# Value products of a pooled attention regrouped from four runs into three, with one block transpose and two copies moved in their queues

## The chip, the cores and the metric

The kernel runs on one core of a Trainium2 chip. The metric is the device time of one execution in microseconds (us). Five engines work side by side, each through its own queue in order: PE (matrix products; its weight loads appear as a row of their own, PEld), DVE (vector), ACT (activation functions), POOL (general), and SP, which here only issues DMAs. They meet through semaphores.

## What is computed

The first stage is attention with pooled queries for 4 batches and 8 heads: 576 queries, 1152 keys, 64 numbers per head. Two mixing stages with matrix products follow, which the change does not touch.

```
q_pool = q.reshape(B, H, S // factor, factor, D).mean(axis=3)
scores = scale * np.matmul(q_pool, k.transpose(0, 1, 3, 2))
scores = scores - np.max(scores, axis=-1, keepdims=True)
attn = np.exp(scores)
attn = attn / (np.sum(attn, axis=-1, keepdims=True) + 1e-09)
return np.matmul(attn, v).astype(np.float32)
...
x = _moe_ref(x=x, **moe_kwargs)
return _moe2_ref(x=x, **moe2_kwargs)
```

## The kernel before, in words

The 32 heads are taken in 16 pairs. A pair has nine **tiles** of 128 query rows by 1152 keys: `TILES` (L277) gives head and block of rows; the fifth tile (index 4) mixes the last 64 rows of both heads. Each tile goes through the same steps:

- `scores` (L291): six products on PE (nine for the mixed tile) into one of two score buffers `SC`, of three PSUM banks each, which the tiles use in turn.
- `smax` (L312): the maximum of each row, on DVE.
- `sexp` (L327): the exponential on ACT, into one of two buffers `e`, with the row sums beside it.
- The exponentials have to be turned, keys onto partitions. Tiles 0 to 3 are turned in blocks on DVE (`turn_blocks`, L351) into the buffer `blk`, and 16 DMAs (`move_blocks`, L357) put the blocks in place in the buffer E. These are the **near** tiles. Tiles 4 to 8, the **far** ones, are turned on PE (`fill`, L382): one block into a bank of the score buffer ("o"), four into the bank TY ("y"), four into the bank TX ("x"). Copies by ACT (o, y) and DVE (x) put them into the buffer M (`take`, L392).
- `pv_part` (L410) multiplies the turned exponentials by the values. The near product of a pair (E, 256 columns) and the far product (M, 320 columns) are nine **parts** each, a part being one product for each head; the trace shows every such product as two PE records, so a part is four records. Each product sums in one PSUM bank, and `pv_copy` (L424) copies the sum out of it on ACT.

The order is written by hand: a loop over **slots** (L657), one for each tile, emits everything, and an engine's queue follows that order. Slot n of a pair emits, for tiles 0 to 3: what `at_gap` has put there, a block transpose, the exponential of tile n+1, what `at_mid` has put there, the scores and then the maximum of tile n+2, the value products of the plan, and what `at` has put there. For tiles 4 to 8 it emits the "o" transpose and its copy, the exponential of tile n+1, the scores of tile n+2, the "y" and "x" transposes, the maximum of tile n+2, and the "x" copy.

So scores run two tiles ahead of the slot and exponentials one. Slots 0 to 3 of a pair also hold the value products of the pair before it: `shares` (L340) sets how many parts lie in which slot. They are emitted behind the scores of tile n+2. In the text below S2 to S8 are the scores of tiles 2 to 8, and S0', S1', S2' those of the next pair's first tiles, which are emitted in slots 7, 8 and (next) 0. One more table, `PREP` (L47), puts the preparation of the next pair's queries and keys (POOL, ACT) and its loads into slots; its entry 'qd' is `q_double` (L256), a copy on ACT.

Of the rest, three steps matter. `norm0` to `norm3` and `spread` invert the row sums (POOL, then a reciprocal and a small transpose on DVE), and send them through device memory to the buffer `rb`; `norm2` (L465) multiplies the value sums by them on POOL, once both copies of `pv_copy` and `rb` are there. Behind `norm2` on POOL stand the low halves of the next pair's keys (`k_lo`, L268), which S0' and S2' read. And on SP's queue the DMAs of `blk` stand behind those of `rb`.

Of the kernel before, what the change touches and what calls it, by code (L numbers as in the profile page):

```python
# [26 lines left out]
NP = NB * NH // 2  # L27
KT = S // 128
# [15 lines left out]
NORM = 9  # L44

PREP1 = ((1, 0, 'kh'), (1, 0, 'qs'), (1, 0, 'qm'), (1, 2, 'qo', 0), (2, 0, 'kt', 0), (2, 2, 'kl', 0, 0), (3, 0, 'kl', 0, 1), (4, 0, 'qo', 1), (4, 2, 'kt', 1), (5, 0, 'kl', 1, 0), (5, 2, 'kl', 1, 1), (5, 2, 'lk'), (5, 2, 'lq'), (5, 2, 'qd', 0), (7, 2, 'qd', 1), (20, 1, 'lv'))
PREP = ((-1, 2, 'qs'), (0, 0, 'qm'), (0, 0, 'qo', 0), (0, 2, 'qo', 1), (1, 1, 'lk'), (1, 1, 'kh'), (2, 0, 'lq'), (2, 1, 'qd', 0), (2, 2, 'kt', 0), (3, 1, 'kt', 1), (3, 1, 'qd', 1), (4, 2, 'kl', 0, 0), (5, 0, 'kl', 0, 1), (6, 0, 'kl', 1, 0), (6, 2, 'kl', 1, 1), (20, 1, 'lv'))  # L47

PIECES = {"a": ((1, 2), ((2, 2), (2, 2), (2, 2)), (9, 2), 14, 15), "x": ((1, 2), ((2, 2), (2, 2), (2, 2)), (3, 2), 5, 7)}
LATE = 5  # L50
# [12 lines left out]
def attn_moe_kernel(ctx: ExitStack, tc: tile.TileContext, qT, kT, vP, muk, mur, wk, wv, wr, wth, wtr, wti, wch, ident, out):  # L63
# [94 lines left out]
    def attention(first):  # L158
# [11 lines left out]
        TX = psV.tile([128, 512], F32, tag="tx", name="tx")  # L170
        TY = psV.tile([128, 512], F32, tag="ty", name="ty")
# [3 lines left out]
        def bank(eng, ins, *banks):  # L175

            ins = ins.ins
            need = []
            for x in banks:
                e, i = owner.get(x, (eng, None))  # L180
                if e != eng and all(i is not y for y in need):
                    need.append(i)
                owner[x] = (eng, ins)
            for e in ("pe", "act", "dve"):
                if e != eng:
                    tc.declare_no_dep(ins, group="sc_" + e, keep=[i for i in need], reason="ordered bank by bank")
            for i in need:
                tc.add_manual_dep(ins, i.name, sync, reason="bank")
            tc.add_to_no_dep_group("sc_" + eng, ins)
# [30 lines left out]
        kts, vns, rss, raws, qs = {}, {}, {}, {}, {}  # L220
# [58 lines left out]
        def quick(P):  # L279
            return P > 0  # L280

        def by_block(n):
            return quick(n // KT) and n % KT < 4
# [3 lines left out]
        def tile_of(n):  # L287
            P, t = divmod(n, KT)
            return (TILES if P else FIRST)[t]
# [22 lines left out]
        def smax(n):  # L312
            m = sm.tile([128, 1], F32, tag="m", name="m")
            if n < THIRDS:

                m3 = sm.tile([128, 4], F32, tag="m3", name="m3")
                for c in range(3):
                    r = dve.tensor_reduce(m3[:, c:c + 1], scs[n][:, c, 0:384], axis=AX.X, op=ALU.max, negate=True)
                    bank("dve", r, (n % 2, c))
                dve.tensor_reduce(m, m3[:, 0:3], axis=AX.X, op=ALU.min)  # L320
                ms[n] = m
                return
            r = dve.tensor_reduce(m, scs[n][:, :, 0:384], axis=AX.XY, op=ALU.max, negate=True)  # L323
            bank("dve", r, *[(n % 2, c) for c in range(3)])
            ms[n] = m

        def sexp(n):  # L327
            P, t = divmod(n, KT)
            if t == 0:
                rss[P] = RS[P % 3]  # L330
            sc, m = scs[n], ms.pop(n)
            e = es_[n] = ep.tile([128, 3, 384], F32, tag="e", name="e", bufs=2)
            x = tile_of(n)
            t = 4 if x is None else 5 * x[0] + x[1]
            r = act.activation(e, sc[:, :, 0:384], AF.Exp, bias=m, scale=1.0, accum_out=rss[P][:, t:t + 1])  # L335
            bank("act", r, *[(n % 2, c) for c in range(3)])
# [3 lines left out]
        def shares(P):  # L340

            if P == NP - 1:
                return ((8, 9),), ((8, 9),)
            return ((9, 5), (10, 4)), ((11, 5), (12, 4))

        pvs = {}

# [3 lines left out]
        def turn_blocks(n):  # L351

            h, t = tile_of(n)
            out = BLK.rearrange("p m (h k t i) -> p h t k m i", h=2, k=KT, t=2)[:, h, t]
            dve.transpose(out, es_[n].rearrange("p a b -> p (a b)").rearrange("p (k m i) -> p k m i", k=KT, m=4))  # L355
# [49 lines left out]
        def take_rest():  # L405
            for n in rest:
                take(n, "y")
            rest.clear()

        def pv_part(k, x):  # L410

            P, g = k
            w = groups[g][1]
            j = (x + 3) % KT
            if x == 0:
                pvs[k] = TX if k == (NP - 1, 0) else TY
            for h in range(2):
                e = Es[k][:, h, j]
                out = pvs[k][64 * h:64 * h + 64, :w]
                if g == 0 and quick(P):  # L420
                    out = out.rearrange("p (a q) -> p a q", a=4)
                pe.matmul(out, lhsT=vns[P][:, h, j], rhs=e, start=(x == 0), stop=(x == KT - 1))  # L422
# [47 lines left out]
        NT = NP * KT  # L470
# [3 lines left out]
        def at(slot, fn, *args):  # L474
            sched.setdefault(slot, []).append((fn, args))
# [3 lines left out]
        def at_mid(slot, fn, *args):  # L479
            mids.setdefault(slot, []).append((fn, args))  # L480
# [3 lines left out]
        def at_gap(slot, fn, *args):  # L484
            gaps.setdefault(slot, []).append((fn, args))
# [3 lines left out]
        for P in range(NP):  # L489
            for g, when in sorted(enumerate(shares(P)), reverse=P == NP - 1):  # L490
                j = 0
                for o, m in when:
                    n = min(P * KT + o, NT)
                    plan.setdefault(n, []).extend(((P, g), j + x) for x in range(m))
                    j += m
                assert j == KT
                if P == NP - 1:
                    at(n, pv_copy, (P, g))
                else:
                    at_gap(n + 1, pv_copy, (P, g))  # L500
            if P == NP - 1:
                for step in (norm0, norm1, norm3):
                    at(NT - 1, step, P)
                at_mid(NT, spread, P)
                at(NT, norm2, P)
            else:
                at(P * KT + NORM, norm0, P)
                at(P * KT + NORM + 1, norm1, P)
                at_mid(P * KT + NORM + 2, norm3, P)
                at(P * KT + NORM + 2, spread, P)  # L510
                at_mid(P * KT + NORM + 4, norm2, P)
            if quick(P):
                at(P * KT + 2, move_blocks, P)

        def run_pv(s):
            for k in plan.pop(s, []):
                pv_part(*k)
# [3 lines left out]
        def prep_sched(P):  # L521
            base = (P - 1) * KT
            for o, hook, name, *args in (PREP if P > 1 else PREP1):
                if P + (name[0] == "l") < NP and (P > 1 or base + o >= 3 or name != "lv"):
# [132 lines left out]
        for s in range(NT + 1):  # L657
            for fn, args in gaps.pop(s, []):
                fn(*args)
            take_rest()  # L660
            if s < NT and by_block(s):
                if s % KT < 3:
                    turn_blocks(s)
                sexp(s + 1)
                if s % KT == 2:
                    turn_blocks(s + 1)
            elif s < NT:
                fill(s, "o")
                take(s, "o")
                if s + 1 < NT:  # L670
                    sexp(s + 1)
            for fn, args in mids.pop(s, []):
                fn(*args)
            if s + 2 < NT:
                scores(s + 2)
            if s < NT and not by_block(s):
                fill(s, "y")
                fill(s, "x")
                rest.append(s)
            if s + 2 < NT:  # L680
                smax(s + 2)
            if s < NT and not by_block(s):
                take(s, "x")
                if s in plan:
                    take_rest()
            run_pv(s)
            for fn, args in sched.pop(s, []):
                fn(*args)
            if s == NT - 1:
                es3.close()  # L690
                next(follow)
                es2.close()
                next(follow)
                next(follow)
            if s == NT:
                next(follow)
                es.close()
                next(follow)
# [494 lines left out]
    with tc.manual_schedule():  # L1193
        dve.memset(hpi, math.pi / 2)
        WR = []
        first = weight_pieces("wr", wr, 512, in_dram, 512) + weight_pieces("wk", wk, 512, in_dram, 512)
        first += weight_pieces("wv", wv, 512, in_dram, 512)[:8 - LATE]
        attention(first)
# [39 lines left out]
```

## Time and profile before

| | |
|---|---|
| time, median of 3 runs | 919.16 us (919.1 to 920.14) |
| the profiled execution | 919.25 us, of which 917.5 us is the span from its first to its last instruction |
| PE busy (modelled) | 901.8 us, 98% of the span |
| PEld, DVE, ACT, POOL busy | 781.5, 688.4, 542.5, 597.4 us (85, 75, 59, 65%) |
| granted PE clock | 0.998 of full speed |
| attention stage | to about 428 us; then the two mixing stages |

PE is put down as busy for nearly the whole span, but the end of a PE record is modelled, and a run of products that waits for something shows it in the starts, not in the busy share. The starts are therefore read below, within one pair. The rows come from the pair whose S2 starts at 239.61 us; the same stretch recurs in 15 pairs.

### The profile page before, as it was taken

The numbers are of one execution on the slowest core, as the hardware profiler recorded it, in microseconds if no ns is written. First come the engines' busy times: TensorE is split into PE (matmuls) and PEld (weight loads), VectorE is DVE, ScalarE is ACT, GpSimd is POOL, SyncE is SP. The second block draws the span as 40 slices with busy tenths as digits, with TensorE's granted clock in tenths as the row PEclk, the third lists the DMA queues.
The fourth block names the chain that finished last, engine by engine and source line by source line (L and its number), as shares of the span: only waits on it lengthen the run. The fifth ranks groups of instructions, "written<-read, shape, count | busy, mean of one in ns | idle before, by whom it ended". The sixth has DMA issues, their size and how long they took to land.

```text
span 917.5 us, 17359 instructions
## 1 busy us (share of the span) xinstructions
PE 901.8 (98%) x6292; PEld 781.5 (85%) x6292; DVE 688.4 (75%) x965; ACT 542.5 (59%) x1133; POOL 597.4 (65%) x662
## 2 busy tenths in 40 slices
PE   8999999999999999999889999999999999999998
PEld 6677777777777777777889999999999999999998
DVE  7888888888888888882589888888758663676712
ACT  7777777777777777764665565555454442443320
POOL 7976777777887777764386565656567475665631
PEclk9999999999999999999999999999999999999999
DMA  7268876777778877659603333333507100010001
GB/s 237 86 180 240 225 211 188 220 215 210 212 207 233 239 208 201 157 166 325 257 2 125 95 103 104 97 99 113 188 1 253 46 27 27 1 53 1 27 26 52
DMA packets 58773, 129.74 MB, mean 141 GB/s; under 512 B 10752, under 2 KB 29888, under 8 KB 58688
## 3 DMA queue, kind: packets, MB, share of 16 engines
q1 hardware_dynamic: 58688, 128.64, 47.1%
q8 instruction: 49, 0.80, 0.4%
q14 instruction: 36, 0.29, 0.1%
HBM read 70.46 MB, written 22.17 MB: 101 GB/s over the span
## 4 chain that ended last, share of the span: by engine, by line
PE 89%; ACT 4%; DVE 3%; POOL 2%; DMA 1%; issue 1%; SPq 0%; DVEq 0%; ACTq 0%; POOLq 0%
PE sc L302 17%; PE ty L422 15%; PE ps L1130 12%; PE ps L852 11%; PE ps L833 10%; PE ps L1149 6%; PE ps L1076 5%; PE ps L802 3%; PE ty L388 3%; PE tx L388 3%; PE sc L388 2%; DVE m L323 1%; ACT e L335 1%; PE ps L1034 1%; DMA rb<-scr 1%
## 5 line engine op out<-in xcount | busy, mean ns | idle before, releaser
L323 DVE TENSOR_REDUCE m<-sc 128x1 f32<-128x1152 f32 x138 | 185.8, 1346 | 48.6 <-PE sc L302 46.8
L335 ACT ACTIVATE e<-sc,m 128x1152 f32<-128x1152 f32 x144 | 176.3, 1225 | 60.8 <-DVE m L323 56.1
L302 PE MATMUL sc<-kt,q 128*128 128x384 f32 (+1 forms) x864 | 192.9, 351 | 3.1 <-ACT M L399 1.7
L302 PEld LDWEIGHTS sc<-kt,q 128*128 128x128 f32 (+1 forms) x864 | 147.1, 191 | 24.0 <-issue 13.8
L1130 PE MATMUL ps<-b,a 128*128 128x288 f32 x816 | 111.2, 295 | 0.0
L1130 PEld LDWEIGHTS ps<-b,a 128*128 128x128 f32 x816 | 109.3, 188 | 0.6
L833 PE MATMUL ps<-x,a 128*128 128x288 f32 x768 | 105.1, 298 | 2.4 <-ACT g L815 2.4
L833 PEld LDWEIGHTS ps<-x,a 128*128 128x128 f32 x768 | 103.7, 191 | 2.7 <-ACT g L815 2.6
L852 PE MATMUL ps<-k,b 128*128 128x288 f32 x768 | 103.5, 295 | 0.0
L852 PEld LDWEIGHTS ps<-k,b 128*128 128x128 f32 x768 | 102.0, 188 | 0.3
L201 POOL TENSOR_TENSOR kt<-kn,kh 64x576 fp32r<-64x576 f32 (+1 forms) x64 | 87.5, 1386 | 2.4
L355 DVE STREAM_TRANSPOSE blk<-e 128x1152 f32<-128x1152 f32 x60 | 81.6, 1360 | 7.4 <-ACT e L335 7.4
L422 PE MATMUL ty<-M,vn 128*64 128x320 f32 x576 | 84.4, 438 | 0.2 <-ACT M L399 0.2
L422 PEld LDWEIGHTS ty<-M,vn 128*64 128x64 f32 x576 | 38.7, 136 | 36.3 <-issue 3.8
L468 POOL TENSOR_TENSOR xt<-xt,rb 128x576 f32<-128x576 f32 x16 | 21.9, 1370 | 73.0 <-ACT xt L432 67.9
L820 POOL TENSOR_TENSOR k<-h,k 128x288 fp32r<-128x288 f32 x64 | 59.1, 939 | 12.4 <-ACT k L819 12.1
L422 PE MATMUL ty<-E,vn 128*64 128x256 f32 x540 | 64.9, 385 | 0.0
L836 DVE TENSOR_TENSOR h<-h 128x288 f32<-128x288 f32 x64 | 42.2, 662 | 21.9 <-ACT h L835 21.2
L1094 ACT ACTIVATE q<-q 128x512 f32<-128x512 f32 x18 | 11.4, 632 | 78.1 <-DVE q L1091 78.1
L802 PE MATMUL ps<-x,blk 128*128 128x288 f32 x384 | 53.3, 296 | 3.4 <-POOL x L782 2.9
L399 DVE COPY M<-tx 128x512 f32<-128x512 f32 x80 | 54.5, 681 | 1.8 <-PE tx L388 1.8
L782 POOL TENSOR_TENSOR x<-t,x 128x288 fp32r<-128x288 f32 x52 | 44.6, 875 | 16.9 <-ACT x L781 16.4
(147 smaller groups left out, 1748.6 us busy)
## 6 DMA issues: line engine op xcount, KB each, us to landing
E<-blk SPq DMA_DIRECT2D x240, 144.0 KB
vn<-vP SPq DMA_DIRECT2D x16, 576.0 KB
kn<-kT SPq DMA_DIRECT2D x15, 576.0 KB
qn<-qT SPq DMA_DIRECT2D x15, 576.0 KB
b<-wtk SPq DMA_DIRECT2D x9, 576.0 KB
rb<-scr SPq DMA_DIRECT2D x32, 144.0 KB
out<-xt SPq DMA_DIRECT2D x32, 144.0 KB
cv<-wk SPq DMA_DIRECT2D x8, 512.0 KB
```

The lines of the kernel that those rows point to most:

```text
L201: engines[e].tensor_tensor(out, x, hi.bitcast(F32), ALU.subtract)
L302: r = pe.matmul(sc[0:m, c, 0:384], lhsT=x, rhs=k[:, 384 * c:384 * c + 384], start=(i == 0), stop=(i == len(ops) - 1),)
L323: r = dve.tensor_reduce(m, scs[n][:, :, 0:384], axis=AX.XY, op=ALU.max, negate=True)
L335: r = act.activation(e, sc[:, :, 0:384], AF.Exp, bias=m, scale=1.0, accum_out=rss[P][:, t:t + 1])
L355: dve.transpose(out, es_[n].rearrange("p a b -> p (a b)").rearrange("p (k m i) -> p k m i", k=KT, m=4))
L388: r = pe.transpose(ps[:, 128 * j:128 * j + 128], flat[:, 128 * k:128 * k + 128], idn)
L422: pe.matmul(out, lhsT=vns[P][:, h, j], rhs=e, start=(x == 0), stop=(x == KT - 1))
L802: pe.matmul(pss[d], lhsT=WR[k][:, w, 128 * d:128 * d + 128], rhs=x[k][:, c], start=(k == 0 and n == 0), stop=(k == 3 and n == 2))
L820: pool.tensor_tensor(q[:, 1], h, q[:, 0].bitcast(F32), ALU.subtract)
L833: pe.matmul(ps, lhsT=WK[k, f // 4][:, w, 128 * (f % 4):128 * (f % 4) + 128], rhs=x[k][:, c], start=(k == 0 and n == 0), stop=(k == 3 and n ...
L852: pe.matmul(pss[d], lhsT=WV[f][:, w, 128 * d:128 * d + 128], rhs=k2[f][:, c], start=(f == 0 and n == 0), stop=(f == 7 and n == 2))
L1130: pe.matmul(pss[d], lhsT=zs[j][z][:, 128 * d:128 * d + 128], rhs=WTK[min(j, 8)][:, w, cs], start=(m == 0 and n == 0), stop=(m == 8 and n = ...
```

## The change

- **Value products.** `shares` gives, for all pairs but the last, near parts 6 and 3 in slots 0 and 1 (5 and 4 before), and far parts 3 and 6 in slots 1 and 2 (5 and 4 in slots 2 and 3 before). Slot 3 has none any more. The far product now sums in bank TX, the near one in TY; before, both used TY. The last pair stays as it was.
- **Copies of the value sums.** `pv_copy` moves from the head of a slot to behind that slot's exponential: the near copy within slot 2, the far copy from slot 4 to slot 3.
- **Third block transpose.** The transpose of tile 2 moves from slot 2 to the end of slot 1, behind the maximum of tile 3.
- **`PREP`.** The second copy of `q_double` moves from the middle of slot 3 to the end of slot 2.

```diff
-PREP = (... (3, 1, 'kt', 1), (3, 1, 'qd', 1), (4, 2, 'kl', 0, 0), ...)
+PREP = (... (3, 1, 'kt', 1), (2, 2, 'qd', 1), (4, 2, 'kl', 0, 0), ...)
...
-            return ((9, 5), (10, 4)), ((11, 5), (12, 4))
+            return ((9, 6), (10, 3)), ((10, 3), (11, 6))
...
-                pvs[k] = TX if k == (NP - 1, 0) else TY
+                pvs[k] = TX if g == (P < NP - 1) else TY
...
-                    at_gap(n + 1, pv_copy, (P, g))
+                    at_mid(n + 1, pv_copy, (P, g))
...
-                if s % KT < 3:
+                if s % KT < 2:
                     turn_blocks(s)
                 sexp(s + 1)
                 if s % KT == 2:
                     turn_blocks(s + 1)
...
             if s + 2 < NT:
                 smax(s + 2)
+            if s < NT and by_block(s) and s % KT == 1:
+                turn_blocks(s + 1)
```

On PE, from the last product of S4 (the mixed tile) to S6, each row is a line, an operation, its output and inputs, and a count; L302 are scores, L422 value products, L388 transposes. Before:

```order
L302 MATMUL sc_120<-kt,q_0_1_125 128x384
L422 MATMUL ty<-M,vn 64x320 x10
L302 MATMUL sc_121<-kt,q_0_0_124 128x384 x6
L422 MATMUL ty<-M,vn 64x320 x8
L388 MATMUL sc_120<-idn,e 128x128
```

The far product lay half before and half behind S5 (the row of six). Now:

```order
L302 MATMUL sc_120<-kt,q_0_1_125 128x384
L422 MATMUL tx<-M,vn 64x320 x12
L302 MATMUL sc_121<-kt,q_0_0_124 128x384 x6
L388 MATMUL sc_120<-idn,e 128x128
L302 MATMUL sc_120<-kt,q_0_0_124 128x384 x6
```

All that is left of the far product lies before S5, and the "o" transpose of tile 4 follows S5 directly. One slot earlier PE now has six near and six far products behind S3, where eight near ones were.

On ACT, from the exponential of tile 3 to that of tile 5 (L335 exponential, L258 `q_double`, L432 copy of a value sum, L399 copy of transposes), before:

```order
L335 ACTIVATE e,rs_138<-sc_120,m 128x1152
L258 CAST q_0_0_124<-q_0_0_124 64x1152
L335 ACTIVATE e,rs_138<-sc_121,m 128x1152
L258 CAST q_0_1_125<-q_0_1_125 64x2x576
L432 COPY xt_69<-ty 128x320
L399 COPY M<-sc_121 128x2x64
L335 ACTIVATE e,rs_138<-sc_120,m 128x1152
```

and now, where the near copy stands behind the first of these exponentials:

```order
L432 COPY xt_69<-ty 128x4x2x32
L258 CAST q_0_0_124<-q_0_0_124 64x1152
L258 CAST q_0_1_125<-q_0_1_125 64x2x576
L335 ACTIVATE e,rs_138<-sc_121,m 128x1152
L432 COPY xt_69<-tx 128x320
L399 COPY M<-sc_121 128x2x64
L335 ACTIVATE e,rs_138<-sc_120,m 128x1152
```

Both `q_double` copies are ahead of the exponential of tile 4, and the copies of value sums are each behind an exponential.

On DVE, from the maximum of tile 3 to that of tile 5 (L323 maximum, L355 block transpose, L446 and L447 the reciprocal and its small transpose, L133 to L141 conversion of a weight), before:

```order
L323 TENSOR_REDUCE m<-sc_120 128x1
L446 RECIPROCAL r_141<-r_141 128x10
L447 STREAM_TRANSPOSE rt<-r_141 128x32
L355 STREAM_TRANSPOSE blk<-e 128x9x4x32 x2
L323 TENSOR_REDUCE m<-sc_121 128x1
L133 TENSOR_SCALAR cv<-cv 128x512
L137 SCALAR_TENSOR_TENSOR cv<-cv 128x512
L141 SCALAR_TENSOR_TENSOR cv<-cv 128x512
L323 TENSOR_REDUCE m<-sc_120 128x1
```

and now:

```order
L323 TENSOR_REDUCE m<-sc_120 128x1
L355 STREAM_TRANSPOSE blk<-e 128x9x4x32
L446 RECIPROCAL r_141<-r_141 128x10
L447 STREAM_TRANSPOSE rt<-r_141 128x32
L355 STREAM_TRANSPOSE blk<-e 128x9x4x32
L323 TENSOR_REDUCE m<-sc_121 128x1
```

The only step that moved on DVE is one block transpose, past the reciprocal and its transpose.

## Rows read from the trace of the kernel before

**Rows 1.** The page's chain that ended last, its shares of the span by engine

```profile
PE 89%; ACT 4%; DVE 3%; POOL 2%; DMA 1%; issue 1%; SPq 0%; DVEq 0%; ACTq 0%; POOLq 0%
```

**Rows 2.** PE in order of time (start, duration, line, count): slot 0's near products

```profile
35.33 2.38 PE L422 MATMUL ty<-E,vn 128*64 128x256 f32 x20
...
394.85 2.38 PE L422 MATMUL ty<-E,vn 128*64 128x256 f32 x20
```

**Rows 3.** PE's weight loads in time order, one pair; in brackets idle time and releaser

```profile
239.61 1.00 PEld L302 LDWEIGHTS sc<-kt,q 128*128 128x128 f32 x6 [0.21 <-POOL qn L237]
240.88 1.92 PEld L422 LDWEIGHTS ty<-E,vn 128*64 128x64 f32 x20 [0.26 <-issue]
243.18 1.00 PEld L302 LDWEIGHTS sc<-kt,q 128*128 128x128 f32 x6 [0.39 <-issue]
244.43 1.49 PEld L422 LDWEIGHTS ty<-E,vn 128*64 128x64 f32 x16 [0.25 <-issue]
246.31 0.19 PEld L302 LDWEIGHTS sc<-kh,qc 128*128 128x128 f32 x1 [0.39 <-issue]
...
248.09 2.35 PEld L422 LDWEIGHTS ty<-M,vn 128*64 128x64 f32 x20 [0.24 <-ACT e L335]
250.94 1.01 PEld L302 LDWEIGHTS sc<-kt,q 128*128 128x128 f32 x6 [0.49 <-issue]
252.21 1.81 PEld L422 LDWEIGHTS ty<-M,vn 128*64 128x64 f32 x16 [0.26 <-issue]
254.51 0.14 PEld L388 LDWEIGHTS sc<-idn,e 128*128 128x128 f32 x1 [0.49 <-issue]
...
255.56 0.54 PEld L388 LDWEIGHTS ty<-idn,e 128*128 128x128 f32 x4
...
265.28 0.47 PEld L302 LDWEIGHTS sc<-kt,q 128*128 128x128 f32 x3 [0.21 <-POOL qn L237]
```

**Rows 4.** PE in order of time: the scores S5 and S0' of the same pair

```profile
250.94 1.34 PE L302 MATMUL sc<-kt,q 128*128 128x384 f32 x6
...
261.00 1.29 PE L302 MATMUL sc<-kt,q 128*128 128x384 f32 x6
```

**Rows 5.** DVE in order of time: maxima of tiles 3, 4, 5 and 0'; transpose of tile 3

```profile
244.56 1.34 DVE L323 TENSOR_REDUCE m<-sc 128x1 f32<-128x1152 f32 x1
...
248.05 1.38 DVE L355 STREAM_TRANSPOSE blk<-e 128x1152 f32<-128x1152 f32 x1 [0.52 <-ACT e L335]
249.35 1.32 DVE L323 TENSOR_REDUCE m<-sc 128x1 f32<-128x1152 f32 x1
...
252.37 1.35 DVE L323 TENSOR_REDUCE m<-sc 128x1 f32<-128x1152 f32 x1
...
262.40 1.36 DVE L323 TENSOR_REDUCE m<-sc 128x1 f32<-128x1152 f32 x1 [0.21 <-PE sc L302]
```

**Rows 6.** ACT in order of time: near copy, exponential 4, far copy, exponentials 5 and 0'

```profile
246.43 0.39 ACT L432 COPY xt<-ty 128x256 f32<-128x256 f32 x1 [1.08 <-PE ty L422]
...
250.76 1.22 ACT L335 ACTIVATE e<-sc,m 128x1152 f32<-128x1152 f32 x1 [1.57 <-DVE m L323]
...
254.63 0.43 ACT L432 COPY xt<-ty 128x320 f32<-128x320 f32 x1 [1.38 <-PE ty L422]
...
255.25 1.22 ACT L335 ACTIVATE e<-sc,m 128x1152 f32<-128x1152 f32 x1
...
263.85 1.23 ACT L335 ACTIVATE e<-sc,m 128x1152 f32<-128x1152 f32 x1 [0.17 <-DVE m L323]
```

**Rows 7.** All engines in order of time, another pair: its exponential 0' and S2'

```profile
109.91 1.22 ACT L335 ACTIVATE e<-sc,m 128x1152 f32<-128x1152 f32 x1 [0.45 <-DVE m L323]
...
111.37 1.28 PE L302 MATMUL sc<-kt,q 128*128 128x384 f32 x6 [0.28 <-ACT e L335]
```

**Rows 8.** POOL in order of time: `norm2` in two pairs, and key halves behind it

```profile
178.52 1.21 POOL L468 TENSOR_TENSOR xt<-xt,rb 128x576 f32<-128x576 f32 x1 [5.09 <-DMA rb<-scr]
...
255.19 1.42 POOL L468 TENSOR_TENSOR xt<-xt,rb 128x576 f32<-128x576 f32 x1 [4.80 <-ACT xt L432]
256.69 2.80 POOL L201 TENSOR_TENSOR kt<-kn,kh 64x576 fp32r<-64x576 f32 x2
```

More of the change, by code (lines that the diff above doesn't have):

```diff
@@ L46 @@
 PREP1 = ((1, 0, 'kh'), (1, 0, 'qs'), (1, 0, 'qm'), (1, 2, 'qo', 0), (2, 0, 'kt', 0), (2, 2, 'kl', 0, 0), (3, 0, 'kl', 0, 1), (4, 0, 'qo', 1), (4, 2, 'kt', 1), (5, 0, 'kl', 1, 0), (5, 2, 'kl', 1, 1), (5, 2, 'lk'), (5, 2, 'lq'), (5, 2, 'qd', 0), (7, 2, 'qd', 1), (20, 1, 'lv'))
-PREP = ((-1, 2, 'qs'), (0, 0, 'qm'), (0, 0, 'qo', 0), (0, 2, 'qo', 1), (1, 1, 'lk'), (1, 1, 'kh'), (2, 0, 'lq'), (2, 1, 'qd', 0), (2, 2, 'kt', 0), (3, 1, 'kt', 1), (3, 1, 'qd', 1), (4, 2, 'kl', 0, 0), (5, 0, 'kl', 0, 1), (6, 0, 'kl', 1, 0), (6, 2, 'kl', 1, 1), (20, 1, 'lv'))
+PREP = ((-1, 2, 'qs'), (0, 0, 'qm'), (0, 0, 'qo', 0), (0, 2, 'qo', 1), (1, 1, 'lk'), (1, 1, 'kh'), (2, 0, 'lq'), (2, 1, 'qd', 0), (2, 2, 'kt', 0), (3, 1, 'kt', 1), (2, 2, 'qd', 1), (4, 2, 'kl', 0, 0), (5, 0, 'kl', 0, 1), (6, 0, 'kl', 1, 0), (6, 2, 'kl', 1, 1), (20, 1, 'lv'))
 PIECES = {"a": ((1, 2), ((2, 2), (2, 2), (2, 2)), (9, 2), 14, 15), "x": ((1, 2), ((2, 2), (2, 2), (2, 2)), (3, 2), 5, 7)}
```

## The prediction

> **What bounds the kernel now.** I began with the page's chain of work that ended last. It gives PE 89% of the span [rows 1], and in the attention stage it names nothing but PE. Taken at its word, only the number and length of PE's records would count. But a chain that ends at modelled PE ends cannot say whether a PE record came late because PE was full or because its input was late. So I went on to the starts: the order in time of PE and of PE's weight loads, then of DVE and ACT, within one pair.
>
> The change touches the 15 stretches in which a pair's slots 0 to 3 carry the value products of the pair before. They are alike: the first near products start at 35.33 us in the first and at 394.85 us in the fifteenth [rows 2], so a pair takes (394.85 - 35.33) / 14 = 25.68 us. I set zero at the start of S2 (239.61) and read the pair up to the next S2 (265.28), 25.67 us later [rows 3].
>
> From S2 to the "o" transpose of tile 4, PE is bound by its own work. Starts follow each other at S2 1.27, 20 near records 2.30, S3 1.25, 16 near 1.88, S4 1.78, 20 far 2.85, S5 1.27, 16 far 2.30 us, in sum 14.90 us [rows 3]. The idle times in brackets there ("issue", 0.25 to 0.49 us) stand at each entry into and exit from a run of value products; there is no other gap.
>
> From then on a loop sets the pace: exponential, transpose "o", scores of two tiles on, their maximum, their exponential. Exponential 5 starts at 15.64 (255.25) and exponential 0', four tiles later, at 24.24 (263.85): twice round the loop in 8.60 us [rows 6]. S2' follows 1.43 us behind exponential 0' [rows 3, 6], because it writes into the score buffer that this exponential reads. The loop is latency from end to end: the maximum starts 0.11 us behind the end of its scores (261.00 + 1.29 to 262.40) [rows 4, 5], and the exponential 1.45 us behind the start of the maximum, idle until then [rows 5, 6]. So the end of a pair is exponential 5 plus 8.60 plus 1.43 us = 10.03 us, and whatever delays exponential 5 should delay the next pair. One pair shows that such a delay is not made up at its end: there exponential 0' waited 0.45 us for its maximum, where the other waited 0.17, and PE then sat idle 0.28 us for that exponential [rows 6, 7].
>
> What holds exponential 5 now? Its maximum starts at 12.76 (252.37) and ends at 14.11, 1.5 us before it is wanted [rows 5, 6]. Exponential 5 stands behind the far copy (254.63) and the "o" copy on ACT, which wait for PE's far products. So the 16 far records behind S5 are what hides the way from S5 through its maximum to its exponential.
>
> **The change, part by part.**
>
> *Value products, PE.* The number of records stays; one run of four goes. From 20 against 16 records, a near record costs (2.30 - 1.88) / 4 = 0.105 us and a far one (2.85 - 2.30) / 4 = 0.1375 us [rows 3]. The new runs are then: 24 near, 2.30 + 0.42 = 2.72; 12 near and 12 far, half of 24 of each, (2.72 + 3.40) / 2 = 3.06; 24 far, 2.85 + 0.55 = 3.40 us. No row shows a run that changes bank in the middle. Between two runs PE shows up to 0.49 us of idle time, and a run without such a gap shows none; I take none, because the weights keep their shape, and keep 0 to 0.3 us for the range.
>
> S5 then starts at 1.27 + 2.72 + 1.25 + 3.06 + 1.78 + 3.40 = 13.48, where it started at 11.33: later by 2.15 us. Behind it nothing is left but the transposes. Scores followed by transposes take 1.05 us from start to start (254.51 to 255.56) [rows 3], so the "o" transpose of tile 4 could start at 14.53, 0.37 us earlier than at 14.90. This is all that PE gains, the one run's entry, exit and first record.
>
> *The exposed way.* S5 ends 1.34 us after its start [rows 4], at 14.82; its maximum starts 0.11 later, at 14.93; exponential 5 starts 1.45 later, at **16.38** instead of 15.64. That is 0.74 us late. PE meanwhile has the "o" transpose, S6 and the "y" and "x" transposes of tile 4, some 2.1 us from 14.53, and then waits.
>
> *Is anything else later than that?* S4 starts at 8.30 instead of 6.70. Its maximum can start some 1.9 us later, at about 10.2 (9.74 before), and its exponential 1.41 us behind that (249.35 to 250.76) [rows 5, 6], at 11.6. It ends at 12.9, 1.6 us before the "o" transpose wants it: hidden. The far copy on ACT comes at about 13.6, since it started 0.12 us behind the end of PE's run [rows 3, 6]; it is done at 14.0, in the time in which ACT waits for maximum 5, and long before the "x" transposes write TX again at about 16.1.
>
> *Near copy.* Before, it held exponential 3: the maximum ended at 245.90 [rows 5], the copy waited until 246.43 for PE [rows 6] and the exponential stood behind it. This goes, worth some 0.7 us to exponential 3 and the 0.52 us for which the transpose of tile 3 waited [rows 5]. But next comes maximum 4, which now waits for S4; so it is worth nothing at the end.
>
> *Third block transpose.* One transpose of 1.3 us passes a reciprocal and a small transpose on DVE, in a stretch where DVE now waits for S4. Worth nothing at the end; the price is in the third rival. *'qd'* takes 1.15 us ahead of exponential 4, in ACT's idle 1.57 us [rows 6]: nothing, as exponential 4 has 1.6 us of cover.
>
> *Sum.* 15 stretches by 0.74 us = 11.1 us. The two later stages begin that much later; the chain there is PE as well [rows 1], and nothing in them is timed from outside, so I take it that nothing is given back. Against the profiled execution's own 919.25 us (917.5 span; the median is 919.16) this makes 930.3 us.
>
> *A rule that speaks the other way.* The rows show idle time of 0.25 to 0.49 us wherever PE goes between 128-column and 64-column weights [rows 3]. The Trainium skill, TensorEngine Tiling (Array Packing), Key Properties, says that changing the tiling mode, not just the tile, drains the engine. The trace agrees with that; by this rule alone the kernel would gain, which is the first rival.
>
> **The rivals.**
>
> *First: PE's own work is the bound throughout.* Then one run less is a pure gain of 0.37 us in each stretch, 15 by 0.37 = 5.6 us, which makes 913.7 us: faster. For it: the chain of PE alone [rows 1] and the idle times at each run [rows 3]. Against it: exponential 5 cannot start before its maximum, and [rows 7]. It decides if the maximum of tile 5 could start by about 14.0, so 0.9 us earlier than I work out.
>
> *Second: the slots of tiles 4 to 8 make most of it up.* Their PE work is about 2.03 us in slots of 2.15 us (four tiles in 8.60). If the loop could be run at the speed of PE's work, five slots would give back 0.6 of the 0.74 us; 15 by 0.14 = 2 us, or 921.4. Between this and the first lies a result of no change. Against it: the loop has no slack in [rows 4 to 6].
>
> *Third: `norm2` comes late too.* The maximum of tile 3 starts at about 5.4 instead of 4.95, as S3 is later, and the transpose put ahead of the reciprocal costs 1.3 us more: `rb` leaves 1.8 us later, with the block DMAs behind it on SP. In one pair `rb` already came last, 0.3 us after the far copy would have released POOL (5.09 against 4.80 us idle) [rows 8], at about 15.9; now that would be 17.7. The key halves behind `norm2` end at 259.49, and S0' starts at 261.00 [rows 4, 8]: 1.5 us of slack, 2.2 with the later S0'. So `norm2` may start at 15.58 + 2.2 = 17.8 before S0' waits. It is hidden by a hair. If `rb` lands later by 0.5 us in every pair, 7.5 us more: 938 us.
>
> **How the numbers follow.** The forecast (0.74 us, with the bank change and the spacing of runs uncertain by about 0.25 us, so 926 to 935 us) has 0.72. The first rival has 0.12, the second 0.10 (half of that within 0.2%), the third 0.06. About 0.2%, 1.8 us, is what a measurement of this kernel can tell from no change. Faster 0.13, same 0.05, slower 0.82. The range 921 to 936 us holds the forecast, the second rival and part of the third, and leaves the first one out.
>
> **What would show it.** In the profile after: three runs of value products with 24 records, and S5 13.5 us behind S2; DVE idle before maximum 5, released by the scores; exponential 5 at 16.4 with ACT idle before it, released by that maximum; PE idle about 1 us before the "o" transpose of tile 5, released by ACT; 26.4 us from S2 to S2'. I would be wrong if S5 came well before 13.5, if the time from exponential 5 to S2' fell under 10.0 us, or if POOL's `norm2` waited for `rb` in most pairs.

## The result, and the profile of the changed kernel

The changed kernel takes 927.69 us (median of 5 runs, 927.55 to 927.75), the kernel before 919.16 us beside it. The ratio is 1.0092 with a 95% interval of 1.0081 to 1.0102: slower by 8.5 us. The profiled execution took 927.55 us, with a span of 925.8 us (917.5 before), at the same granted clock of 0.998. Nearly every touched pair now takes 26.20 to 26.24 us, where it took 25.66. 15 times 0.57 us is the 8.5 us. One execution of a kernel below (six far parts behind S5) took 1766.32 us, nearly twice its other three, and is left out of all comparisons as slow; no trace of it was kept.

The page still gives PE nearly the whole chain, as in [rows 1], with three points moved to ACT and DVE. First the busy times, then the chain's shares:

```profile
PE 897.3 (97%) x6292; PEld 784.2 (85%) x6292; DVE 688.9 (74%) x965; ACT 543.9 (59%) x1133; POOL 596.6 (64%) x662
...
PE 87%; ACT 6%; DVE 4%; issue 1%; POOL 1%; DMA 0%; SPq 0%; ACTq 0%; DVEq 0%
```

The view that sums up idle time by releaser says more. Its columns are engine, output and line of the instruction that waited, what released it, the sum in us, the number of waits and the longest.

```profile
ACT e L335 <- DVE m L323: 80.4, 105, 3.3
...
DVE m L323 <- PE sc L302: 60.3, 85, 1.5
POOL xt L468 <- DMA rb<-scr: 58.8, 11, 7.1
...
PEld sc L388 <- ACT e L335: 21.2, 34, 1.7
```

Before, these four sums were 56.1, 46.8, 5.1 and 3.2 us. So exponentials now wait longer for maxima, maxima for scores, and PE's "o" transposes for exponentials. These three are the links of one loop. `norm2` waits for `rb` too; whether that costs anything is a question for the experiments.

Within one pair, the counterpart of [rows 3] in PE's weight loads (start, duration, engine, line, operation, output<-input, count, and in brackets the idle time before with its releaser). S2 starts at 244.02 us, which is zero from here on:

```profile
244.02 0.99 PEld L302 LDWEIGHTS sc<-kt,q 128*128 128x128 f32 x6 [0.24 <-issue]
245.27 2.36 PEld L422 LDWEIGHTS ty<-E,vn 128*64 128x64 f32 x24 [0.25 <-issue]
248.01 1.00 PEld L302 LDWEIGHTS sc<-kt,q 128*128 128x128 f32 x6 [0.38 <-issue]
249.25 1.06 PEld L422 LDWEIGHTS ty<-E,vn 128*64 128x64 f32 x12 [0.25 <-issue]
250.39 1.44 PEld L422 LDWEIGHTS tx<-M,vn 128*64 128x64 f32 x12
252.32 0.19 PEld L302 LDWEIGHTS sc<-kh,qc 128*128 128x128 f32 x1 [0.49 <-ACT e L335]
252.43 0.36 PEld L302 LDWEIGHTS sc<-kt,q 128*64 128x64 f32 x2
252.78 0.19 PEld L302 LDWEIGHTS sc<-kh,qc 128*128 128x128 f32 x1
...
254.09 2.89 PEld L422 LDWEIGHTS tx<-M,vn 128*64 128x64 f32 x24 [0.24 <-issue]
257.48 1.00 PEld L302 LDWEIGHTS sc<-kt,q 128*128 128x128 f32 x6 [0.49 <-ACT e L335]
258.46 0.14 PEld L388 LDWEIGHTS sc<-idn,e 128*128 128x128 f32 x1
...
261.65 0.14 PEld L388 LDWEIGHTS sc<-idn,e 128*128 128x128 f32 x1 [1.06 <-ACT e L335]
...
270.25 1.00 PEld L302 LDWEIGHTS sc<-kt,q 128*128 128x128 f32 x6 [0.24 <-POOL qn L237]
```

There are three runs of 24 records (the second of 12 and 12, with no gap where the bank changes at 250.39), then S5 at 13.46, the "o" transpose of tile 4 directly behind it at 14.44, and the next S2 at 26.23. Before the "o" transpose of tile 5 (261.65) PE stands idle for 1.06 us until an exponential is done.

The mark in the last row names an instruction of POOL (L237), as two of [rows 3] do, and POOL is busy almost without a break from `norm2` up to it. It does not set the pace, however. Its counterpart one pair earlier

```profile
242.72 1.41 POOL L237 TENSOR_TENSOR qn<-qn 128x576 f32<-128x576 f32 x1
```

lasts to 244.13, and S2 had started at 244.02. From the start of exponential 0' to S2', on the other hand, it is 1.42 or 1.43 us in every one of these pairs.

Which exponential is seen on DVE and on ACT, the counterparts of [rows 5] and [rows 6]; DVE first, the maxima of tiles 4, and of 5 and 6:

```profile
254.21 1.36 DVE L323 TENSOR_REDUCE m<-sc 128x1 f32<-128x1152 f32 x1 [0.59 <-PE sc L302]
...
258.83 2.62 DVE L323 TENSOR_REDUCE m<-sc 128x1 f32<-128x1152 f32 x2 [1.48 <-PE sc L302]
```

Then ACT: exponential 4, the far copy, exponential 5, exponential 0':

```profile
255.66 1.22 ACT L335 ACTIVATE e<-sc,m 128x1152 f32<-128x1152 f32 x1 [0.90 <-DVE m L323]
...
257.60 0.43 ACT L432 COPY xt<-tx 128x320 f32<-128x320 f32 x1 [0.63 <-PE tx L422]
...
260.29 1.22 ACT L335 ACTIVATE e<-sc,m 128x1152 f32<-128x1152 f32 x1 [1.08 <-DVE m L323]
...
268.82 1.22 ACT L335 ACTIVATE e<-sc,m 128x1152 f32<-128x1152 f32 x1 [0.20 <-DVE m L323]
```

In [rows 6] exponential 5 had no wait of its own; now ACT is idle for 1.08 us before it (260.29, which is 16.27 from zero), and the maximum of tile 5 lets it go. That maximum waited 1.48 us for S5. The chain of waits, cut to this stretch, now leaves PE there, which it did not do before. In order of time, each step with start, duration and engine:

```profile
254.17 3.38 PE tx L422 x24
257.55 1.26 PE sc L302 x6
258.81 0.02 issue
258.83 1.37 DVE m L323
...
260.29 1.32 ACT e L335 x2
261.61 0.04 issue
261.65 0.33 PE sc L388
```

The far run, S5, its maximum, its exponential and the "o" transpose follow each other with nothing beside them. Behind the attention stage nothing changed: the last 497 us of both spans hold the same 3518 PE records, with PE busy for 487.95 us before and 487.97 us after.

### The profile page after: what moved, and what is told of

Same layout as the page of the kernel before. It is cut to its first block, busy times and chain, and to the rows that moved or that the text cites. A ratio compares the mean times of both kernels' runs of the same rounds, so it can differ in the third digit from the quotient of the medians.

```text
span 925.8 us, 17360 instructions
## 1 busy us (share of the span) xinstructions
PE 897.3 (97%) x6292; PEld 784.2 (85%) x6292; DVE 688.9 (74%) x965; ACT 543.9 (59%) x1133; POOL 596.6 (64%) x662
## 4 chain that ended last, share of the span: by engine, by line
PE 87%; ACT 6%; DVE 4%; issue 1%; POOL 1%; DMA 0%; SPq 0%; ACTq 0%; DVEq 0%
PE sc L302 16%; PE ps L1132 12%; PE ps L854 11%; PE ps L835 10%; PE tx L422 9%; PE ty L422 7%; PE ps L1151 6%; PE ps L1078 5%; PE ps L804 3%; PE ty L388 3%; ACT e L335 3%; PE tx L388 3%; DVE m L323 3%; PE sc L388 1%; PE ps L1036 1%
## 5 line engine op out<-in xcount | busy, mean ns | idle before, releaser
L323 DVE TENSOR_REDUCE m<-sc 128x1 f32<-128x1152 f32 x138 | 185.4, 1353 | 63.5 <-PE sc L302 60.3
L335 ACT ACTIVATE e<-sc,m 128x1152 f32<-128x1152 f32 x144 | 176.1, 1223 | 82.2 <-DVE m L323 80.4
L302 PE MATMUL sc<-kt,q 128*128 128x384 f32 (+1 forms) x864 | 190.4, 351 | 3.7 <-ACT M L399 1.7
L302 PEld LDWEIGHTS sc<-kt,q 128*128 128x128 f32 (+1 forms) x864 | 145.6, 188 | 24.7 <-issue 7.7
L355 DVE STREAM_TRANSPOSE blk<-e 128x1152 f32<-128x1152 f32 x60 | 81.5, 1358 | 0.0
L422 PE MATMUL tx<-M,vn 128*64 128x320 f32 x540 | 78.5, 435 | 0.0
L422 PE MATMUL ty<-E,vn 128*64 128x256 f32 x540 | 64.9, 385 | 0.0
L422 PEld LDWEIGHTS tx<-M,vn 128*64 128x64 f32 x540 | 37.4, 137 | 32.2 <-issue 3.7
L784 POOL TENSOR_TENSOR x<-t,x 128x288 fp32r<-128x288 f32 x52 | 44.6, 875 | 17.8 <-ACT x L783 17.3
L399 DVE COPY M<-tx 128x512 f32<-128x512 f32 x80 | 54.5, 681 | 1.8 <-PE tx L388 1.8
```

The costliest lines, as they stand in the source:

```text
L302: r = pe.matmul(sc[0:m, c, 0:384], lhsT=x, rhs=k[:, 384 * c:384 * c + 384], start=(i == 0), stop=(i == len(ops) - 1),)
```

## The experiments

The theory: nothing of the far product is left behind S5 to cover the 2.81 us from S5 to exponential 5 (13.46 to 16.27), and the saved run is still worth 0.37 us a pair if something covers them. The rivals: the moved copies and transpose cost the time; the late `rb` costs it; the change of banks costs it; or the removed run is worth nothing.

### How much of the far product lies behind S5

Starting from the changed kernel, one, three or all six of the far parts of slot 2 go behind S5 again (slot 3), with the far copy behind them, ahead of the "o" copy. With all six moved, the number of runs stays three; with one or three there are four runs, as before the change. The far copy goes along with the parts here; in the experiment after this one it stays where the change has put it.

```diff
-            return ((9, 6), (10, 3)), ((10, 3), (11, 6))
+            return ((9, 6), (10, 3)), ((10, 3), (12, 6))
...
-                    at_mid(n + 1, pv_copy, (P, g))
+                    (at_gap if g else at_mid)(n + 1, pv_copy, (P, g))
```

The smaller doses end in `(11, 3), (12, 3)))` and `(11, 5), (12, 1)))`. Expected with all six, three and one:

> The changed kernel, with the six far parts of slot 2 moved behind S5 into slot 3, so three runs of value products, in slots 0, 1 and 3; the far copy stands at the head of slot 4, as in the kernel before. Theory (the way S5, maximum 5, exponential 5 is exposed in the changed kernel): S5 starts at about 10.1 us behind S2, its maximum and exponential are ready by 14.7, and the o transpose of tile 4 comes at 14.5 instead of 14.9; exponential 5 at 15.3. The saved run then is a gain: 25.3 us per pair, 0.37 us less than before, 913.6 us. Rival (the two-bank products, the moved transpose or the late rb cost the time): no faster than the changed kernel, about 927 us. Rival (PE was never short of a run): about 919 us.

> The changed kernel, with the six far parts of slot 2 split, three in slot 2 and three in slot 3 behind S5, so four runs again; far copy at the head of slot 4. Theory (exposed way): S5 at 11.9 us, chain ready at 14.7, exponential 5 held by PE at 15.6 as in the kernel before: 25.66 us per pair, 919 us. Rival (banks, moved transpose or rb): 927 us.

> The changed kernel, with one far part of slot 2 moved behind S5 into slot 3 (five stay); far copy at the head of slot 4. Theory (exposed way): S5 at 12.9 us, exponential 5 by its maximum at 15.74, by PE and the copies at 15.64, so the two ends nearly meet: 25.7 to 25.8 us per pair, 919.5 to 921 us. Rival (banks, moved transpose or rb): 927 us, as none of these is changed.

Measured, with the period of a typical pair:

| far parts behind S5 | runs of value products | time, us | ratio to before | pair, us |
|---|---|---|---|---|
| 0 (the change) | 3 | 927.69 | 1.0092 [1.0081, 1.0102] | 26.23 |
| 1 | 4 | 920.36 | 1.0011 [1.0002, 1.0021] | 25.72 |
| 3 | 4 | 917.31 | 0.9979 [0.9969, 0.9988] | 25.52 |
| 6 | 3 | 914.26 (913.62 to 915.27) | 0.9945 [0.9928, 0.9962] | 25.17 |
| before: 4 | 4 | 919.16 | 1 | 25.66 |

One part of nine, 0.55 us of products, takes back 7.3 of the 8.5 us. In that kernel S5 starts at 12.91 and exponential 5 at 15.75, 2.84 us later, so the way itself is as long as before; it only begins earlier:

```profile
255.62 1.22 ACT L335 ACTIVATE e<-sc,m 128x1152 f32<-128x1152 f32 x1 [0.16 <-DVE m L323]
```

(its S2 starts at 239.87). Its wait for the maximum is down to 0.16 us: the way is all but covered. With six parts behind S5 it is covered, and the pair is shorter than before the change. A typical pair of that kernel, S2 at 261.48, weight loads of PE: the far run behind S5, the "o" transpose of tile 4, and the last S2.

```profile
272.64 2.89 PEld L422 LDWEIGHTS tx<-M,vn 128*64 128x64 f32 x24 [0.25 <-issue]
276.02 0.14 PEld L388 LDWEIGHTS sc<-idn,e 128*128 128x128 f32 x1 [0.49 <-issue]
...
286.67 0.99 PEld L302 LDWEIGHTS sc<-kt,q 128*128 128x128 f32 x6
```

And its maximum and exponential of tile 5:

```profile
274.74 1.35 DVE L323 TENSOR_REDUCE m<-sc 128x1 f32<-128x1152 f32 x1
```

```profile
276.62 1.24 ACT L335 ACTIVATE e<-sc,m 128x1152 f32<-128x1152 f32 x1
```

The "o" transpose starts at 14.54, where PE's own work alone had been put at 14.53; exponential 5 follows at 15.14 and waits for nothing; the pair ends at 25.19. A pair of before had 14.90, 15.64 and 25.67. So the removed run is worth 0.36 us on PE, and exponential 5 gains 0.50 us. The other 0.14 us do not come from the run. From the "o" copy to exponential 5 ACT takes 0.16 us here and 0.15 with only the transpose and `q_double` moved, in a kernel further below; it takes 0.30 before, and also in the last kernel of this section, which has these three runs without the moves. So this head start goes with the moved transpose and `q_double`.

Three pairs of this kernel are longer, by 0.2 to 0.4 us. One is the third pair, which is 0.25 to 0.3 us longer in every kernel here, the kernel before among them. Another (S2 at 235.88), first DVE, then POOL, then ACT:

```profile
247.35 1.35 DVE L133 TENSOR_SCALAR cv<-cv 128x512 uint32<-128x512 uint32 x1
...
250.08 1.35 DVE L323 TENSOR_REDUCE m<-sc 128x1 f32<-128x1152 f32 x1
```

```profile
246.04 2.38 POOL L198 TENSOR_SCALAR kt<-kn 64x1152 fp32r<-64x1152 f32 x2
```

```profile
251.52 1.22 ACT L335 ACTIVATE e<-sc,m 128x1152 f32<-128x1152 f32 x1 [0.39 <-DVE m L323]
```

The first step of a weight conversion (L133) took 1.35 us beside a POOL instruction, where it takes 0.42 us in the typical pair (272.95, POOL idle). Maximum 5 stands behind it on DVE, at 14.20 instead of 13.26, and exponential 5 waited 0.39 us for it.

### The maximum alone

The changed kernel, with the maximum of each pair's tile 5 taken in three pieces, one for each bank of the scores, as the kernel already does for its first tiles. The order on PE is untouched.

```diff
-            if n < THIRDS:
+            if n < THIRDS or (n > KT and n % KT == 5):
```

> The changed kernel, but the maximum of tile 5 of each pair but the first is taken bank by bank (three reductions of 0.55 us and one of 0.16 us instead of one of 1.36), so that two thirds are done while S5 still runs. More work on DVE, PE and ACT as in the changed kernel. Theory (exposed way): the maximum is ready about 0.6 us earlier, exponential 5 at about 15.7 instead of 16.27; 25.65 us per pair, 918.5 to 920 us. Rival (banks, moved transpose, rb or anything on PE): 927.7 us or more, as only DVE work is added.

Measured: 922.09 us (921.88 to 922.25), ratio 1.003 [1.0018, 1.0041], pair 25.86 us. The loss shrank from 8.5 to 2.8 us, less than expected. In order of time: S5 among the weight loads, then the pieces on DVE, then exponential 5 on ACT.

```profile
254.42 1.00 PEld L302 LDWEIGHTS sc<-kt,q 128*128 128x128 f32 x6 [0.49 <-ACT e L335]
```

```profile
255.08 1.49 DVE L318 TENSOR_REDUCE m<-sc 128x1 f32<-128x384 f32 x3 [0.28 <-PE sc L302]
256.60 0.15 DVE L320 TENSOR_REDUCE m<-m 128x1 f32<-128x3 f32 x1
```

```profile
256.85 1.22 ACT L335 ACTIVATE e<-sc,m 128x1152 f32<-128x1152 f32 x1 [0.70 <-DVE m L320]
```

From S5 to exponential 5 it is 2.43 us, where it was 2.81. The first piece could begin only 0.66 us behind the start of S5, and the four instructions took 1.67 us against 1.36 for one, so 0.38 us were won and not 0.57. The pair became 0.37 us shorter. This is the plainest evidence for the theory: an edit that touches nothing but the way from S5 to exponential 5 moves the pair one to one.

### The parts of the change alone

From the kernel before, three times: the new shares and banks with copies, transpose and `q_double` where they were; the third transpose and `q_double` moved and nothing else; the far sum in bank TX and nothing else. And the changed kernel with the third transpose put back into slot 2.

```diff
-            return ((9, 5), (10, 4)), ((11, 5), (12, 4))
+            return ((9, 6), (10, 3)), ((10, 3), (11, 6))
...
-                pvs[k] = TX if k == (NP - 1, 0) else TY
+                pvs[k] = TX if g == (P < NP - 1) else TY
```

> The kernel before with only the value products changed: three runs (six near; three near and three far; six far) and the far sum in TX; the copies of value sums, the third block transpose and the second q_double copy stay where they were, so the far copy stands ahead of exponential 4, at the head of slot 3. Theory (exposed way from S5): exponential 4 is held by the far copy until about 13.9 us, so the o transpose of tile 4 comes at 15.2 instead of 14.5, but exponential 5 still comes with its maximum at 16.3: 927 to 929 us, the whole loss. Rival (the moved copies or transpose cause the loss): near 919 us. Rival (the far copy ahead of exponential 4 adds to it): 930 us or more.

> The kernel before with only the third block transpose moved to the end of slot 1 and the second q_double copy to the end of slot 2. Theory: nothing on the path, since PE sets the pace of slots 0 to 3 there and S5's way stays hidden behind 16 far records: 919 us. Rival (rb leaves later, norm2 and the keys behind it hold S0'): up to 927 us.

> The kernel before with only the far sum moved from bank TY to TX; four runs, the copies where they were. Theory: 919 us, the x transposes of tile 4 start a microsecond after the far copy is done. Rival (the two banks cost something on PE, or TX holds the transposes): slower by over 0.2%, above 921 us.

> The changed kernel with only the third block transpose back in slot 2, behind the reciprocal. Theory: 927.7 us as the changed kernel, with POOL waiting for rb less often, since DVE waits for S4 there in any case. Rival (the late rb is part of the loss): faster by over 0.2%, below 926 us.

| kernel | time, us | ratio to before | `rb` came last for `norm2` |
|---|---|---|---|
| shares and banks alone | 933.55 | 1.0154 [1.0137, 1.017] | |
| transpose and `q_double` alone | 918.76 | 0.9996 [0.9987, 1.0006] | 4 times |
| banks alone | 918.3 | 0.9991 [0.9981, 1.0] | |
| the change, transpose put back | 927.57 | 1.0093 [1.0078, 1.0108] | 11 times |

The moved transpose and `q_double` cost nothing, and neither does the change of banks. With the transpose put back, `rb` comes last 11 times as in the change, and not less often, as I had expected. But it comes in earlier: over the 15 pairs `norm2` starts at 14.42 in the median, where the change has 15.63. In a pair of this kernel with S2 at 244.96:

```profile
259.22 1.42 POOL L468 TENSOR_TENSOR xt<-xt,rb 128x576 f32<-128x576 f32 x1 [3.88 <-DMA rb<-scr]
```

The time stays as it was (927.57 against 927.69 us), so the late `rb` costs nothing, either. In the changed kernel, `norm2` and the key halves behind it, on POOL, and S0' on PE:

```profile
260.02 1.40 POOL L468 TENSOR_TENSOR xt<-xt,rb 128x576 f32<-128x576 f32 x1 [5.06 <-DMA rb<-scr]
261.50 2.80 POOL L201 TENSOR_TENSOR kt<-kn,kh 64x576 fp32r<-64x576 f32 x2
```

```profile
265.89 1.06 PEld L302 LDWEIGHTS sc<-kt,q 128*128 128x128 f32 x6
```

The key halves end at 264.30, 1.6 us before S0' starts. `norm2` starts at 16.0 here and between 14.6 and 16.3 in all 15 pairs, well under the 17.8 at which, as worked out, S0' would have to wait.

The first kernel is a miss: I expected 927 to 929 us, and it is 933.55, worse than the whole change. There the far copy stands behind the far run but ahead of exponential 4 in ACT's queue, and the second `q_double` behind that. From a pair with S2 at 248.15, on ACT:

```profile
261.73 0.43 ACT L432 COPY xt<-tx 128x320 f32<-128x320 f32 x1 [4.01 <-PE tx L422]
262.05 1.23 ACT L335 ACTIVATE e<-sc,m 128x1152 f32<-128x1152 f32 x1
...
263.39 1.15 ACT L258 CAST q<-q 64x1152 fp32r<-64x1152 f32 x1
264.45 0.25 ACT L399 COPY M<-sc 128x128 f32<-128x128 f32 x1
264.73 1.23 ACT L335 ACTIVATE e<-sc,m 128x1152 f32<-128x1152 f32 x1
```

ACT waits 4.01 us at the far copy; exponential 4 starts at 13.90 as I had worked out. What I had overlooked is that `q_double` then stands between it and the "o" copy, so that exponential 5 comes at 16.58. The wait grows from there: exponential 6 starts at 18.71, against 18.16 in the change. So the new places of the copies and of `q_double` do matter once all far products lie ahead of S5: they save about 6 us of what would be a loss of 14.

### Without the moves, and a better version

Three kernels side by side: all far parts of slot 2 behind S5, once more; the same with a weight conversion's steps on DVE (L133 to L141) one slot later, out of the way of maximum 5; and from the kernel before only the shares and the banks, copies and transpose left where they were.

```diff
-PIECES = {"a": ((1, 2), ((2, 2), (2, 2), (2, 2)), (9, 2), 14, 15), ...}
+PIECES = {"a": ((1, 2), ((3, 2), (3, 2), (3, 2)), (9, 2), 14, 15), ...}
```

> The same kernel as d6_far_behind_s5, timed in more rounds: 913.6 to 915.3 us, as its three undisturbed runs were.

> d6 (far parts behind S5) with the three DVE steps of the weight conversion moved from slot 2 to slot 3, behind maximum 5. In d6 three pairs of fourteen were 0.2 to 0.4 us longer; in the one read, the first of these steps took 1.35 us instead of 0.42 beside a POOL step, maximum 5 came 0.9 us late, and exponential 5 waited for it. Theory: those pairs lose their extra time, about 0.9 us in all: 913.0 to 914.3 us. Rival (the steps now delay maximum 6): 916 us or more.

> The kernel before with only the value products changed as in d6: near parts 6 and 3 in slots 0 and 1, far parts 3 in slot 1 and 6 in slot 3 behind S5, far sum in TX; copies, block transpose and q_double as before the change. Theory: the near copy ahead of exponential 3 costs nothing, since S5 needs exponential 3 only at 10.1 us and it ends by 8.4; the second q_double copy ends at 14.1, before the far copy: 913 to 915.5 us, so the moves of copies and transpose are not needed. Rival (they are needed, as beside p_products_alone): 917 us or more.

| kernel | time, us | ratio to before | pair, us |
|---|---|---|---|
| far run behind S5, again | 913.19 (912.22 to 914.07) | 0.9928 [0.9916, 0.9941] | 25.17 |
| and conversion a slot later | 912.82 (912.32 to 913.28) | 0.9925 [0.9913, 0.9938] | 25.17 |
| shares and banks only | 912.98 (912.88 to 914.65) | 0.9928 [0.9914, 0.9941] | 25.22 |

All three are faster than both kernels, by 6.2 to 6.6 us against the kernel before, and their medians lie 0.02 to 0.4 us under the ranges expected. The first is the kernel that had 914.26 us above, with 919.32 beside it. Moving the conversion leaves one longer pair, the third, where there were two or three, which is too little to tell its time from the others. The last kernel is the cheapest to make: one line of shares and one of banks. With the far run behind S5 none of the moved copies or transposes is needed.

## Why the prediction was right, and where its sizes were off

The forecast was 930.3 us, and it is 927.69: slower, by the mechanism that it names, and 2.6 us less than it says. Its steps, in order:

- **The new runs.** 2.72, 3.06 and 3.40 us were worked out; 2.74, 3.07 and 3.39 are measured. The bank change in mid-run costs nothing. S5 was put at 13.48 and starts at 13.46. This step held.
- **The exposed way.** Exponential 5 was put at 16.38 and starts at 16.27. Two terms were too long. S5 lasts 1.31 us and not 1.34, and the maximum starts 0.04 us behind its end, not 0.11: I had taken that distance from S0', at another place of the pair. The 1.45 us from the maximum to the exponential are 1.46.
- **The loop behind it.** From exponential 5 to 0' it is 8.53 us where 8.60 were carried over. Its first turn takes 4.23 us, the second 4.30. This is no sign that lost time is made up, as the second rival had it: with only the banks changed, where exponential 5 comes at 15.6 and not late, the first turn takes 4.23 us too. Why it is shorter was not tested. From exponential 0' to S2' it is the 1.43 us of before.
- **The sum.** S2' was put at 26.41 and comes at 26.23. Of the 0.18 us, 0.02 went at S5, 0.03 and 0.07 between S5 and its maximum, 0.07 in the loop, and 0.01 came back at the exponential. 15 by 0.18 us = 2.7 us is the whole difference. Nothing was made up in the later stages.
- **What hides.** Maximum 4 at 10.19 (10.2 worked out), exponential 4 at 11.64 (11.6), the far copy at 13.58 (13.6): hidden, as said. Transpose and `q_double` are worth nothing alone, as said and as a run shows. The near copy was not moved alone; with the far run behind S5, the kernels with and without all these moves differ by 0.2 us.

The **first rival** had the right amount on the wrong bound. A run less does save 0.36 us on PE, as the "o" transpose at 14.54 with the far run behind S5 shows. The Trainium skill, TensorEngine Tiling (Array Packing), Key Properties, says that a change of the tiling mode drains the engine. The 0.36 us for one entry, exit and first record less fit that, but they do not show that the mode is the cause. The prediction's "wherever PE goes between 128-column and 64-column weights" is too wide: within S4, PE goes from 128 to 64 columns and back with no idle time (252.32, 252.43 and 252.78 above); in these rows such gaps stand at the ends of the runs of value products. The gain is lost because, where the far run stands ahead of S5, exponential 5 cannot start in time to use it.

The **third rival's** condition came true without its price: `rb` came last in 11 of 15 pairs, but `norm2` started by 16.3 and not at 17.7. So the text was wrong to name "`norm2` waiting for `rb` in most pairs" as a sign against the forecast. It happened, and proves nothing, since the limit was a start at 17.8, not a wait. The 1.8 us that were added are about right: the small transpose ahead of `rb` (L447) starts at 8.12 (252.14), where it started at 6.45 (246.06). What was wrong is the 15.9 to which they were added. That was the one pair of before in which `rb` came last; in the other 14 it came earlier than the far copy let `norm2` start, by how much was not read.

One small thing stays open. With only the banks changed a pair takes 25.57 us, and with only the transpose and `q_double` moved 25.60, both a little under the 25.66 of before with the same four runs. The kernel with three far parts behind S5 has both changes and four runs, and takes 25.52, about both gains together. So of the 0.49 us of the kernel with six parts behind S5, the removed run is worth about 0.35 (25.52 to 25.17), which is close to the 0.37 of the prediction, and these two changes the rest. What makes their part was not tested.

## What to carry to other kernels

A run of work that looks free to move may be the cover of a latency beside it: before moving it, ask which instruction's input is produced just ahead of it, and write down how long the way through the other engines takes (here 2.81 us from scores to exponential). When runs are merged, merge them on the side that keeps this cover; the same three runs cost 8.5 us on one side of S5 and go with a gain of about 6 us on the other, some 5 of it the removed run (15 by 0.35). And a wait that grows is a cost only if the start that it delays passes the point where someone else waits for it.

## What was not expected of the hardware

A 128x512 uint32 `TENSOR_SCALAR` on DVE (L133), 0.42 us long in most pairs, took 1.35 us where it began while POOL ran a `TENSOR_SCALAR` of 64x1152 (L198). It ended at 248.70, 0.28 us behind the end of the POOL instruction at 248.42, as if it had got little done until then. In the kernel with the maximum in three pieces it began 0.65 us before the end of the POOL instruction, took 0.92 us, and ended 0.27 us behind it:

```profile
252.42 0.92 DVE L133 TENSOR_SCALAR cv<-cv 128x512 uint32<-128x512 uint32 x1
```

```profile
250.68 2.39 POOL L198 TENSOR_SCALAR kt<-kn 64x1152 fp32r<-64x1152 f32 x2
```

The Trainium skill, GPSIMD Engine Reference, Specifications, says that the GpSimd engine shares its SBUF interfaces with VectorE, and names contention with some kinds of DVE instruction. These rows agree that the two engines can hold each other up; whether L133 is of the kinds named no trace here shows. In the kept traces 21 other L133 steps began 0.19 us or more before the end of such a POOL instruction, and all ended 0.27 to 0.29 us behind it. Not every DVE instruction is slowed: the maximum just ahead (246.08, in the pair with S2 at 235.88) ran beside the same POOL instruction in its usual 1.36 us. It is a cost that no order of either engine's queue shows: only where the two meet in time did it come up, and here it lay ahead of the maximum on which the pair depended.
